# The order in which a scheduled two-layer MLP kernel is written out: TensorE's steps at their planned end

## The chip, the cores and the metric

The kernel runs on one core of a Trainium2 chip. What counts is the device time of one launch in microseconds (us). Five engines work side by side: TensorE (PE in the profile; PEld is its loading of weights), VectorE (DVE), ScalarE (ACT), GpSimd (POOL), and SyncE (SP), which issues the DMAs here.

## The reference

Sliding-window attention feeds two MLPs, one after the other, all in fp32:

```python
scores = scale * (q @ k.T)                 # 4 x 8 heads, 576 positions, head size 64
attn = softmax(scores where 0 <= i - j < 64)
x = (attn @ v) as (2304, 512)
h = x @ w_in                               # layer 0: 512 x 2048
x = (s * relu(h)**2 + b) @ w_out           # 2048 x 512
h = x @ w_in2                              # layer 1
out = (max(h, 0) + alpha * min(h, 0)) @ w_out2
```

What the title calls two layers, the code numbers 0 and 1; the words "layer one" of the change mean the first of them.

## The kernel before

Every fp32 operand is split into a high and a low part, and each product is the sum of three matmuls (high by high, high by low, low by high). So weights are converted on the chip: `converted` loads a piece (`raw`, L676), and ScalarE (L680, L684) and VectorE (L689, L690, L694, L699) split it; `weight_pair` forms sums of weights (L797 to L800) and stages them (L706, L708, L711); `weight` makes the pieces of w_out (ScalarE L769, VectorE L772, GpSimd L764 for a running sum that serves the bias, whose matmuls are L782).

The hidden units are handled in groups: five in layer 0, (0,0) to (0,4), four in layer 1. The tokens are taken in three pieces of 768, each as two halves of 384 columns. From group (0,2) on, `hidden_pair` computes two blocks of hidden units by two halves of tokens with seven products instead of eight (a scheme like Strassen's). Each `product` is six matmuls of 128x384 (L1016). The results lie in PSUM: b1 and b4 are tiles of the pool "h", and T["hb"] is one tile of two banks, "ab" in the profile, half 0 for b2 and half 1 for b3. The copies between them (L1027) are ScalarE's, and `total` (VectorE, L1047 in layer 0, L1049 in layer 1) reads both halves of "ab":

```python
product(6, 2, b2_, hb2, False)
product(2, 3, b1_, b1, False)
copy(b3_, b2_, [hb2], [hb3], 2)
product(7, 4, b3_, hb3, False)
product(3, 5, b2_, hb2, False)
copy(b4_, b3_, [hb3], [b4], 4)
product(4, 6, b4_, b4, False)
```

`project` multiplies the activated blocks by w_out into four PSUM banks y0 to y3 (L1507), and `sums` brings a group's result into the running sum `ay` in SBUF. There are two ways: VectorE adds y to ay (L1601); or, for those m that `CARRIED` names, ScalarE copies ay into the bank before the group (L1500), TensorE accumulates on it, and ScalarE copies it back (L1594).

The order of all this is planned. Each piece of work is a step of `Plan`, with the ways (engine and cost) in which it can be done, what it reads and writes, a due time `at`, and an earliest time. `emit` takes the steps one after the other as a list scheduler does: per engine it plans a start and an end from the costs, and calls the step's function at once, so the program is written in the order of planned starts. The tile framework then derives every wait between engines from the order in which the program was written: of two steps on one tile, with one of them writing it, the later written one waits for the earlier. The queue of each engine runs in its own written order. The due times of conversions done ahead of their group come from `EARLY_AT` and `OUT_AT` and the line in `ahead`.

Of the kernel before, what the change touches and what calls it, by code (L numbers as in the profile page):

```python
# [2 lines left out]

# [28 lines left out]
EARLY = (4, 2, 0, 3, 1, 1, 0)  # L32
# [8 lines left out]
LAG = 1.7  # L41
SEVEN = ((1, 1), (1, 2), (1, 3))
OUT_EARLY = {(0, 3): (0,), (0, 4): (1, 2), (1, 0): (3,), (1, 1): (4,), (1, 2): (5,)}
OUT_AT = {(0, 3): (32.0,), (0, 4): (27.4, 76.1), (1, 0): (53.8,), (1, 1): (27.3,), (1, 2): (51.8,)}
EARLY_AT = {0: (2.3, 28.5, 91), 1: (0,), 2: (39.8,)}
AHEAD2 = 30.0
IDLE = 0.0
PAIRS_ACT = 430.0
CARRIED = {(0, 2): (1,3,), (0, 3): (1,3,), (0, 4): (1,3,)}
LAG7, FORM = 2.3, 10.0  # L50
SOON7 = {(1, 1): (0.0, 0.0, 0.0), (1, 2): (0.0, 0.0, 0.0), (1, 3): (0.0, 0.0, 12.0)}
SOON = 16.0
# [30 lines left out]
class Plan:  # L83
# [100 lines left out]
    def emit(self):  # L184
        n = len(self.steps)
        after = [[] for _ in range(n)]
        for i, (_, deps, _, first, _) in enumerate(self.steps):
            for d in deps + first:
                after[d].append(i)
        path = [0.0] * n  # L190
        for i in range(n - 1, -1, -1):
            cost = min(w[1] + w[3] for w in self.steps[i][0])
            path[i] = cost + max((path[j] + 0.1 for j in after[i]), default=0.0)
        rank = [(-self.steps[i][2], path[i]) for i in range(n)]

        def hop(a, b):

            if a == b:
                return 0.0 if a == "pe" else 0.12
            return 0.2 if "pe" in (a, b) else 0.1  # L200

        took = {}
        left = [len(s[1]) + len(s[3]) for s in self.steps]
        done = [0.0] * n
        free = {"sp": 0.7, "dve": 2.2, "pool": 0.75, "act": 2.0, "pe": 1.1}
        pool_from = 0.0
        ready = {i for i in range(n) if left[i] == 0}
        order = []
        while ready:
            cands = []  # L210
            for i in ready:
                ways, deps, _, _, after_ = self.steps[i]
                best = None
                for w in ways:
                    share = len(w) > 4
                    w = w[:4]
                    t = max((done[d] + hop(took[d], w[0]) for d in deps), default=0.0)
                    t = max(t, free.get(w[0], 0.0), after_)
                    if w[0] == "pe" and t < self.SLOW:
                        w = (w[0], w[1] * 2, w[2], w[3])  # L220
                    if w[0] == "sp" and t < self.SLOW_DMA:
                        w = (w[0], w[1] * self.DMA_FACTOR, w[2], w[3])
                    if share:
                        w = (w[0], w[1] + 0.8 * max(0.0, min(free["pool"], t + w[1]) - max(t, pool_from)), w[2], w[3])
                    value = t + w[1] * (1.0 + self.SPARE[w[0]]) + w[3]
                    if best is None or value < best[0]:
                        best = (value, t, w)
                cands.append((best[1], i, best[2]))
            t0, i0, b0 = min(cands, key=lambda c: (c[0], self.steps[c[1]][2], c[1]))
            t0, i0, b0 = max(  # L230
                (c for c in cands if c[2][0] == b0[0] and c[0] <= t0 + self.WINDOW),
                key=lambda c: (rank[c[1]], -c[1]),
            )
            eng, cost, fn, tail = b0
            free[eng] = t0 + cost
            if eng == "pool":
                pool_from = t0
            done[i0] = t0 + cost + tail
            took[i0] = eng
            ready.remove(i0)  # L240
            order.append((t0, eng))
            fn()
            for j in after[i0]:
                left[j] -= 1
                if left[j] == 0:
                    ready.add(j)
        assert len(order) == n
        return max(done)


@with_exitstack
def tile_window_attention_two_mlps(
# [92 lines left out]
    for g in range(SPLIT[0]):  # L345
        for bi in range(NB):
            n = blocks[bi][1]
            took = len(groups[0][g]) * 24 * n * 0.000444
# [12 lines left out]
    with tc.manual_schedule():  # L361
# [415 lines left out]
        def bias(at):  # L777
            ps = T.tile("bias", h_ps, [P, 512], F32, "h", 2)

            def mms():  # L780
                for m in range(NK):
                    nc.tensor.matmul(T[ps][:, m:m + 1], wsum[:, m * P:(m + 1) * P], b_sb[:, 0:1], start=True, stop=True)  # L782

            T.step([("pe", 1.5, mms, 0.0)], reads=["wsum", "b"], writes=[ps], at=at)
            T.step([dve(NK, lambda: nc.vector.tensor_copy(ybias, T[ps][:, :NK]))], reads=[ps], writes=["ybias"], at=at)
# [54 lines left out]
        def weight_load(n, at):  # L840
            for k in (0, 2, 3, 1):
                lo, hi = PIECES[k]
                w = w_slot(n, k)
                for h in "hl":
                    T.parts[f"{w}.{h}"] = w
                T.step(
                    dma(1, P * (hi - lo) * W2 * 8, lambda w=w, lo=lo, hi=hi: nc.sync.dma_start(
                        out=f32(T[w]), in_=wd[n, :, 2 * lo * W2:2 * hi * W2])),
                    reads=[f"wd.{n}.{k}"], writes=[f"{w}.h", f"{w}.l"], at=at,
                )  # L850
# [689 lines left out]
        def carried(m, layer, g):  # L1540
            return (layer, g) in CARRIED and m in CARRIED[layer, g]

# [69 lines left out]
        for bi in range(NB):  # L1612
            for hp in range(0, NHP, 2 if bi == 0 else 1):
# [4 lines left out]
                else:  # L1618
                    t = begin[0, 0, bi - 1] + (hp / NHP) * (begin[0, 0, bi] - begin[0, 0, bi - 1]) - LEAD
                    at1, at2 = t, t + 1.0  # L1620
                before, after = group(hp // 2 if bi == 0 else bi * NHP + hp, bi, (hp, hp + 1) if bi == 0 else (hp,), at1, at2)
# [26 lines left out]
        for g in range(SPLIT[0]):  # L1648
            for i, f in enumerate(groups[0][g]):
                for part in range(2):  # L1650
                    at = FIRST_W[2 * i + part] if g == 0 else begin[0, g, 0] + (i + 2 * part) * pace[g, 0] - 12.0
# [23 lines left out]
        for x, (layer, g) in enumerate(order_of):  # L1675
            fs = groups[layer][g]
            t = begin[layer, g, turns[layer, g][0]]
            took = NQ * len(fs) / 2 * PAIR
            for p in range(len(fs) // 2):
                n = number[layer, g, p]  # L1680
                at = t + p * PAIR
                if x == 0:
                    weight_pair(n, 0, fs[2 * p], fs[2 * p + 1], at - 20.0, at - 20.0 - AHEAD, True)
                else:
                    weight_load(n, at - 10.0)
            end = layer == 0 and g == len(groups[0]) - 1
            for i, f in enumerate(fs if (layer, g) not in SEVEN else ()):
                at = t + LAG * PAIR + i * PAIR / 4 - 12.0 - 15.0 * end
                weight(layer, f, 1, at, at - AHEAD)
            def ahead():  # L1690
                nonlocal early
                for e in range(EARLY[x]):
                    layer_, g_, p_ = next(k for k, v in number.items() if v == early)
                    at = t + (EARLY_AT[g][e] if layer == 1 else 25.0 + e * took / EARLY[x])
                    weight_pair(
                        early, layer_, *groups[layer_][g_][2 * p_:2 * p_ + 2], at + IDLE * (x > 0),
                        at - (AHEAD2 if layer == 1 and g else 30.0), False, (layer, g) in SEVEN,
                    )
                    early += 1

            def ahead_out():
                if layer == 1:
                    staging.more = 2 * NMAX
                for p, since in zip(OUT_EARLY.get((layer, g), ()), OUT_AT.get((layer, g), ())):
                    out_pair(p, t + since + IDLE, t + since - AHEAD2, (layer, g) in SEVEN)

            if (layer, g) != (1, 0):
                ahead_out()
                ahead()
            if (layer, g) in SEVEN:  # L1710
                seven(layer, g)
                continue
            for q in turns[layer, g]:
                for p in range(len(fs) // 2):
                    hidden_pair(layer, g, q, p)
                if end and q == turns[layer, g][0]:
                    bias(t + PAIR)
                for c in range(2):
                    for i in range(len(fs)):
                        project(layer, g, 2 * q + c, i)  # L1720
                    sums(layer, g, 2 * q + c)
            if (layer, g) == (1, 0):
                ahead()
                ahead_out()
# [55 lines left out]
```

## Time and profile before

| | us |
|---|---|
| median of 3 runs | 842.01 (841.2 to 842.93) |
| the profiled execution | 841.64 |
| its span in the trace | 839.6 |
| TensorE busy | 821.4 (98%) |
| VectorE busy | 702.6 (84%) |
| ScalarE busy | 555.2 (66%) |

The span runs from the first to the last instruction of the trace; the rest of an execution's time lies around it. Busy time counts overlapping instructions of one engine once. A matmul's row gives its time from entry to end; since the next one enters before the last one has ended, the pace of a stream is read from start to start.

### The profile page before, as it was taken

What the parts mean: (1) busy time and instruction counts of PE and PEld (TensorE: products, weight loads), DVE (VectorE), ACT (ScalarE), POOL (GpSimd) and SP (SyncE); (2) the same over time, 40 slices, a digit from 0 to 9 for tenths busy, and PEclk for the clock granted to TensorE, in tenths of its full rate; (3) what the DMA queues carried; (4) which work ended last, traced back from release to release, by engine and by line L of the source; (5) the groups of instructions that cost most, each with busy time, mean ns of one, the idle gap of its engine ahead of it and who ended that gap; (6) DMA issues with size and microseconds to landing.
All of it is one profiled execution on the core that took longest, in us unless ns stands there. A gap on an engine that the chain in (4) does not pass through costs nothing.

```text
span 839.6 us, 15049 instructions
## 1 busy us (share of the span) xinstructions
PE 821.4 (98%) x5481; PEld 768.6 (92%) x5485; DVE 702.6 (84%) x1195; ACT 555.2 (66%) x1249; POOL 105.4 (13%) x117
## 2 busy tenths in 40 slices
PE   7899999999999999999999999999999999999998
PEld 4688887888899999999999999999989999999998
DVE  6977899698995698789949898978799988888695
ACT  6777997644575576778748677775566566656461
POOL 6542355532100001001000000000000000000000
PEclk9999999999999999999999999999999999999999
DMA  8575976476648999989698676998785599469813
GB/s 284 185 231 153 283 229 197 164 261 242 236 170 324 368 342 368 405 311 369 249 388 300 259 314 246 333 363 304 278 301 187 211 328 346 131 212 350 319 47 114
DMA packets 81258, 224.61 MB, mean 268 GB/s; under 512 B 8096, under 2 KB 33824, under 8 KB 81184
## 3 DMA queue, kind: packets, MB, share of 16 engines
q1 hardware_dynamic: 81184, 223.65, 74.2%
q8 instruction: 43, 0.70, 0.3%
q14 instruction: 31, 0.25, 0.1%
HBM read 154.67 MB, written 68.94 MB: 266 GB/s over the span
## 4 chain that ended last, share of the span: by engine, by line
PE 69%; DVE 13%; DMA 12%; ACT 3%; issue 1%; POOL 1%; SPq 0%; DVEq 0%; ACTq 0%; POOLq 0%
PE y L1507 16%; PE h L1016 14%; PE y L1299 13%; PE ab L1016 11%; PE h L1417 7%; DMA raw<-w_out 4%; PE y L1477 3%; DMA raw<-w_in 3%; DMA vd<-al 2%; DVE raw L694 1%; PE ab L531 1%; PE y L636 1%; PE y L605 1%; DVE raw L699 1%; DVE raw L690 1%
## 5 line engine op out<-in xcount | busy, mean ns | idle before, releaser
L1016 PE MATMUL h<-ax,aw 128*128 128x384 f32 x936 | 184.4, 335 | 2.0 <-ACT h L1027 1.2
L1016 PEld LDWEIGHTS h<-ax,aw 128*128 128x128 f32 x936 | 163.9, 188 | 4.1 <-ACT h L1027 1.8
L1507 PE MATMUL y<-ax,woh 128*128 128x384 f32 x672 | 153.9, 335 | 2.3 <-DVE ay L1601 1.8
L1016 PE MATMUL ab<-ax,aw 128*128 128x384 f32 x702 | 139.9, 335 | 1.1 <-ACT ab L1027 0.6
L1016 PEld LDWEIGHTS ab<-ax,aw 128*128 128x128 f32 x702 | 122.9, 188 | 3.0 <-ACT ab L1027 1.6
L1507 PEld LDWEIGHTS y<-ax,woh 128*128 128x128 f32 x672 | 119.3, 188 | 4.2 <-DVE ay L1601 3.3
L1507 PE MATMUL y<-ax,wol 128*128 128x384 f32 x336 | 95.0, 334 | 0.0
L1417 PE MATMUL h<-ax,aw 128*128 128x512 f32 (+1 forms) x360 | 84.3, 377 | 0.8 <-DVE ax L654 0.7
L1417 PEld LDWEIGHTS h<-ax,aw 128*128 128x128 f32 x360 | 61.9, 189 | 12.4 <-DVE ax L654 1.6
L1299 PE MATMUL y<-ax,woh 128*128 128x384 f32 (+1 forms) x273 | 61.7, 333 | 0.0
L1507 PEld LDWEIGHTS y<-ax,wol 128*128 128x128 f32 x336 | 61.5, 188 | 0.0
L1128 ACT ACTIVATE al<-h 128x384 f32<-128x384 f32 (+2 forms) x58 | 30.1, 519 | 40.0 <-PE h L1417 21.6
L680 ACT ACTIVATE raw<-raw 128x512 f32<-128x512 f32 x56 | 37.5, 674 | 21.8 <-DMA raw<-w_in 14.2
L588 POOL TENSOR_TENSOR as__83<-as__83,den 128x512 f32<-128x512 f32 x36 | 41.5, 1173 | 59.9 <-DVE den L581 37.0
L1299 PEld LDWEIGHTS y<-ax,woh 128*128 128x128 f32 x273 | 48.4, 188 | 0.3 <-ACT y L1313 0.3
L1323 DVE TENSOR_TENSOR ay<-y,ay 128x384 f32<-128x384 f32 (+1 forms) x73 | 39.3, 546 | 10.5 <-PE y L1299 6.6
L764 POOL TENSOR_TENSOR al<-al,raw 128x512 f32<-128x512 f32 x15 | 21.8, 1450 | 193.4 <-DVE raw L699 193.4
L694 DVE SCALAR_TENSOR_TENSOR raw<-raw 128x512 int32<-128x512 int32 x56 | 42.9, 773 | 2.9 <-ACT raw L684 2.7
L1299 PE MATMUL y<-ag,wol 128*128 128x384 f32 x192 | 43.9, 335 | 0.4 <-DVE ag L711 0.4
L1313 ACT COPY y<-y 128x384 f32<-128x384 f32 x54 | 25.1, 465 | 27.7 <-PE y L1299 24.2
L1145 ACT ACTIVATE aq<-aq,slope 128x384 f32<-128x384 f32 x48 | 27.2, 610 | 23.9 <-DVE aq L1049 23.8
L570 ACT ACTIVATE as__83<-as__83,nm 128x128 f32<-128x128 f32 x96 | 37.3, 392 | 4.7 <-DVE nm L556 4.5
(189 smaller groups left out, 1670.9 us busy)
## 6 DMA issues: line engine op xcount, KB each, us to landing
ax<-xd SPq DMA_DIRECT2D x91, 768.0 KB, 6.8
aw<-wd SPq DMA_DIRECT2D x33, 512.0 KB, 5.3
xd<-ax SPq DMA_DIRECT2D x21, 768.0 KB, 4.1
raw<-w_in SPq DMA_DIRECT2D x28, 512.0 KB, 5.7
raw<-w_out SPq DMA_DIRECT2D x28, 512.0 KB, 5.6
wd<-ag SPq DMA_DIRECT2D x27, 512.0 KB, 5.0
xd<-aq SPq DMA_DIRECT2D x12, 768.0 KB, 4.2
xd<-ax SPq DMA_DIRECT2D x36, 192.0 KB, 4.7
```

The source lines that it names most:

```text
L570: nc.scalar.activation(sm3()[:, x, :], S_(h)[:, i * P:(i + 1) * P] if summed else sm3()[:, x, :], AF.Exp, bias=T[nm][:, x:x + 1], scale=sc ...
L588: eng.tensor_mul(x, x, d)
L680: [act(512, lambda: nc.scalar.activation(T[t], H().bitcast(F32), AF.Abs, scale=65536.0))],
L694: [dve(512, lambda: nc.vector.scalar_tensor_tensor(out=L(), in0=H(), scalar=-0x80000000, in1=L(), op0=ALU.bitwise_and, op1=ALU.bitwise_or) ...
L1016: nc.tensor.matmul(bank(), W[:, wj, a, kt * P:(kt + 1) * P], X[:, c, kt, :], start=start and kt == 0 and y == 0, stop=kt == 1 and y == 2, ...
L1128: T.step([act(n, lambda: nc.scalar.activation(rn(), hn(), AF.Relu)), dve(n, lambda: nc.vector.tensor_scalar_max(rn(), hn(), 0.0))], reads= ...
L1145: T.step([act(HALF, lambda: nc.scalar.activation(r2n(), hn(), AF.Identity, scale=slope[:, f:f + 1]))], reads=[hk, "side"], writes=[r2], at ...
L1299: nc.tensor.matmul(v(to)[:, c], W[:, s, a * P:(a + 1) * P], G[:, h, c], start=start and p == 0 and y == 0, stop=p == 1 and y == 2, skip_gr ...
L1323: [dve(e.stop - e.start, lambda: nc.vector.tensor_add(T[k][:, e], v(x)[:, e], T[k][:, e]))],
L1417: nc.tensor.matmul(T[ps][:, :n].rearrange("p (c t) -> p c t", t=P), T[w][:, k * P:(k + 1) * P], T[X(x, k)], start=st, stop=sp,)
L1477: nc.tensor.matmul(T[Y(m)][:, :n], T[w[a]][:, m * P:(m + 1) * P], T[gx[c]], start=(x == 0 and j == 0), stop=(x == len(fs) - 1 and j == 2),)
L1507: nc.tensor.matmul(ps, T[w][:, m * P:(m + 1) * P], T[x], start=(i == 0 and j == 0 and not carried(m, layer, g)), stop=(last and j == 2), s ...
```

## The change

It has three parts. `emit` no longer calls a step's function when it picks it, but hands the picked steps to the new `write`. That keeps each engine's own order, and writes the steps in the order of a key: for a step on TensorE its planned end, for all others their planned start. Group (0,2) leaves `CARRIED`, so its y1 and y3 are added by VectorE too. And the due times of weights and w_out pieces that are converted ahead take other values.

```diff
-OUT_AT = {(0, 3): (32.0,), (0, 4): (27.4, 76.1), (1, 0): (53.8,), (1, 1): (27.3,), (1, 2): (51.8,)}
-EARLY_AT = {0: (2.3, 28.5, 91), 1: (0,), 2: (39.8,)}
+OUT_AT = {(0, 3): (27.2,), (0, 4): (24.0, 77.8), (1, 0): (76.9,), (1, 1): (28.4,), (1, 2): (48.2,)}
+EARLY_AT = {0: (14.4, 32.7, 83.6), 1: (0,), 2: (22.3,)}
...
-CARRIED = {(0, 2): (1,3,), (0, 3): (1,3,), (0, 4): (1,3,)}
+CARRIED = {(0, 3): (1,3,), (0, 4): (1,3,)}
...
             order.append((t0, eng))
-            fn()
+            picked.append((i0, b0))
             for j in after[i0]:
                 left[j] -= 1
                 if left[j] == 0:
                     ready.add(j)
         assert len(order) == n
+        self.write(picked, [t for t, _ in order], after)
         return max(done)
+
+    def write(self, picked, begins, after):
+
+        left = [len(s[1]) + len(s[3]) for s in self.steps]
+        then, last, way, key = {}, {}, {}, {}
+        for (i, b), t in zip(picked, begins):
+            way[i] = (t, b)
+            key[i] = t + b[1] if b[0] == "pe" else t
+            if b[0] in last:
+                then[last[b[0]]] = i
+                left[i] += 1
+            last[b[0]] = i
+        heap = [(key[i], i) for i in way if left[i] == 0]
+        heapq.heapify(heap)
+        count = 0
+        while heap:
+            _, i0 = heapq.heappop(heap)
+            t0, (eng, cost, fn, _) = way[i0]
+            count += 1
+            fn()
+            for j in after[i0] + ([then[i0]] if i0 in then else []):
+                left[j] -= 1
+                if left[j] == 0:
+                    heapq.heappush(heap, (key[j], j))
+        assert count == len(way)
...
-                    at = t + (EARLY_AT[g][e] if layer == 1 else 25.0 + e * took / EARLY[x])
+                    at = t + (EARLY_AT[g][e] if layer == 1 else 15.0 + e * took / EARLY[x])
```

The lines of the new kernel from `hidden_pair` on are 28 higher than those of the old one (L1016 becomes L1044). On TensorE there are as many instructions as before, on GpSimd and SP too; VectorE has 15 more and ScalarE 27 fewer. The order is the same up to about 235 us of the old run, and nearly so after about 600 us.

TensorE, at the first pair of that stretch (238 us of the old run): products 7 and 3 on the two halves of "ab", then the next products on "h" tiles, with the queues whose signal each waits for. Before:

```order
L1016 MATMUL ab_2557<-ax_78,aw_80 128x384 [waits DMAHW5_49,Activation_49]
L1016 MATMUL ab_2557<-ax_78,aw_80 128x384 x5
L1016 MATMUL ab_2557<-ax_78,aw_80 128x384 [waits DMAHW7_49]
L1016 MATMUL ab_2557<-ax_78,aw_80 128x384 x5
L1016 MATMUL h_2801<-ax_78,aw_80 128x384 [waits Activation_49]
L1016 MATMUL h_2801<-ax_78,aw_80 128x384 x5
L1016 MATMUL h_2727<-ax_78,aw_80 128x384 [waits DMAHW0_49,Activation_49]
```

And of the changed kernel:

```order
L1044 MATMUL ab_2557<-ax_78,aw_80 128x384 [waits DMAHW5_49,Activation_49]
L1044 MATMUL ab_2557<-ax_78,aw_80 128x384 x5
L1044 MATMUL ab_2557<-ax_78,aw_80 128x384 [waits DMAHW7_49,Activation_49]
L1044 MATMUL ab_2557<-ax_78,aw_80 128x384 x5
L1044 MATMUL h_2799<-ax_78,aw_80 128x384 x6
L1044 MATMUL h_2728<-ax_78,aw_80 128x384 [waits DMAHW0_49]
```

The order of TensorE is the same; product 3 waits for ScalarE now, and the two products behind it no longer do.

VectorE, at the sums of the second half of group (0,2) (277 us of the old run; L797 to L800 form sums of weights, L708 and L711 stage them). Before, where y1 and y3 go by ScalarE:

```order
L800 TENSOR_TENSOR as__83<-raw_84,as__83 128x256
L711 TENSOR_TENSOR ag_81<-raw_84,ag_81 128x256
L708 CAST ag_81<-as__83 128x2x256
L1118 CAST ax_78<-al_86 128x384
L1601 TENSOR_TENSOR ay_79<-y0_3008,ay_79 128x384
L1121 TENSOR_TENSOR ax_78<-al_86,ax_78 128x384
L1601 TENSOR_TENSOR ay_79<-y2_3016,ay_79 128x384
```

And of the changed kernel:

```order
L739 TENSOR_TENSOR ag_81<-raw_84,ag_81 128x256
L736 CAST ag_81<-as__83 128x2x256 x2
L739 TENSOR_TENSOR ag_81<-as__83,ag_81 128x2x256 x2
L1629 TENSOR_TENSOR ay_79<-y0_3012,ay_79 128x384
L1629 TENSOR_TENSOR ay_79<-y1_3016,ay_79 128x384
L1149 TENSOR_TENSOR ax_78<-al_86,ax_78 128x384
L1629 TENSOR_TENSOR ay_79<-y2_3021,ay_79 128x384
L1629 TENSOR_TENSOR ay_79<-y3_3025,ay_79 128x384
```

The half's four sums stand close together, and a burst of weight steps stands ahead of them in both orders, a longer one in the new.

SP, the DMA queue at the beginning of that stretch (raw is a load of weights, ax one of a layer's input, wd a store of staged weights). Before:

```order
L676 DMA raw_84<-w_in1 128x1024 x2
L979 DMA ax_78<-xd_87 128x1536 x7
L823 DMA wd_89<-ag_81 128x1024
L823 DMA wd_89<-ag_81 128x512
L823 DMA wd_89<-ag_81 128x1024 x2
L676 DMA raw_84<-w_in1 128x1024 x3
```

And of the changed kernel:

```order
L704 DMA raw_84<-w_in1 128x1024 x2
L1007 DMA ax_78<-xd_87 128x1536
L851 DMA wd_89<-ag_81 128x1024
L704 DMA raw_84<-w_in1 128x1024
L1007 DMA ax_78<-xd_87 128x1536 x4
L851 DMA wd_89<-ag_81 128x512
L851 DMA wd_89<-ag_81 128x1024 x2
```

A load of weights that stood behind the seven loads of ax and four stores is now ahead of most of them.

## Rows read from the trace of the kernel before

**Rows 1.** The page: its head and its first part, the busy time by engine.
```profile
span 839.6 us, 15049 instructions
...
PE 821.4 (98%) x5481; PEld 768.6 (92%) x5485; DVE 702.6 (84%) x1195; ACT 555.2 (66%) x1249; POOL 105.4 (13%) x117
```

**Rows 2.** The table by stretch: start:end and length, then each engine's busy time (instructions), clock granted.
```profile
235.00:332.00 97.00, 95.21 (x541) 93.49 (x540) 74.67 (x142) 59.34 (x120) 3.98 (x3) 1.00 0.87 324
235.00:835.20 600.20, 594.42 (x3400) 587.37 (x3398) 501.29 (x874) 388.35 (x756) 9.48 (x7) 1.00 0.78 287
```

**Rows 3.** Timeline of PE around 238 us: start, busy time, operation, count, [idle before, releaser].
```profile
237.48 2.24 PE L1016 MATMUL ab<-ax,aw 128*128 128x384 f32 x12
239.56 1.37 PE L1016 MATMUL h<-ax,aw 128*128 128x384 f32 x7
```

**Rows 4.** Timeline of ACT in that stretch.
```profile
239.75 0.46 ACT L1027 COPY h<-ab 128x384 f32<-128x384 f32 x1 [1.02 <-PE ab L1016]
```

**Rows 5.** Timeline of PE, 390 to 396 us.
```profile
390.22 1.21 PE L1016 MATMUL ab<-ax,aw 128*128 128x384 f32 x6
391.98 1.31 PE L1016 MATMUL h<-ax,aw 128*128 128x384 f32 x6 [0.55 <-ACT h L1027]
...
394.29 0.61 PE L1507 MATMUL y<-ax,woh 128*128 128x384 f32 x2 [0.48 <-DVE ay L1601]
...
395.44 0.95 PE L782 MATMUL h<-b_sb,al 128*128 128x1 f32 x8
396.25 0.59 PE L1507 MATMUL y<-ax,woh 128*128 128x384 f32 x2
```

**Rows 6.** Timeline of ACT at 391 us.
```profile
391.46 0.46 ACT L1027 COPY h<-ab 128x384 f32<-128x384 f32 x1 [1.07 <-PE ab L1016]
```

**Rows 7.** Timeline of PE around 18 us.
```profile
18.69 1.90 PE L636 MATMUL y<-ay 128*64 128x64 f32 x56
```

**Rows 8.** Timeline of ACT and of DVE around 21 us.
```profile
20.86 0.38 ACT L649 CAST ax<-y 128x256 fp32r<-128x256 f32 x1
...
21.27 0.42 DVE L650 CAST ax<-y 128x256 fp32r<-128x256 f32 x1
```

**Rows 9.** Timeline of all engines at the end.
```profile
834.86 0.50 PE L1299 MATMUL y<-ax,wol 128*128 128x192 f32 x3
...
835.20 0.50 PE L1299 MATMUL y<-ax,woh 128*128 128x192 f32 x3
...
836.07 0.62 DVE L1323 TENSOR_TENSOR ay<-y,ay 128x192 f32<-128x192 f32 x2 [0.76 <-PE y L1299]
```

**Rows 10.** Timeline of PE, 276 to 280 us and 326 us.
```profile
276.05 1.21 PE L1016 MATMUL ab<-ax,aw 128*128 128x384 f32 x6
277.46 0.61 PE L1507 MATMUL y<-ax,woh 128*128 128x384 f32 x2 [0.21 <-ACT y L1500]
...
279.92 0.35 PE L1507 MATMUL y<-ax,woh 128*128 128x384 f32 x1
...
326.69 0.61 PE L1507 MATMUL y<-ax,woh 128*128 128x384 f32 x2 [1.35 <-DVE ay L1601]
```

**Rows 11.** Timeline of DVE, 276 to 279 us.
```profile
276.81 0.42 DVE L711 TENSOR_TENSOR ag<-raw,ag 128x256 fp32r<-128x256 f32 x1
...
277.75 0.55 DVE L1601 TENSOR_TENSOR ay<-y,ay 128x384 f32<-128x384 f32 x1
```

**Rows 12.** Groups of ACT by line, 235 to 332 us: busy, mean ns, idle before.
```profile
L680 ACT ACTIVATE raw<-raw 128x512 f32<-128x512 f32 x10 | 6.7, 669 | 5.2 <-DMA raw<-w_in 5.2
...
L1500 ACT COPY y<-ay 128x384 f32<-128x384 f32 x12 | 5.5, 496 | 1.3 <-DVE ay L1559 1.2
L1594 ACT COPY ay<-y 128x384 f32<-128x384 f32 x10 | 4.8, 475 | 0.1
```

**Rows 13.** Groups of DVE by line, the same stretch.
```profile
L1601 DVE TENSOR_TENSOR ay<-y,ay 128x384 f32<-128x384 f32 x10 | 5.4, 549 | 11.6 <-PE y L1507 11.6
```

**Rows 14.** The chain that ended last, 235 to 332 us: start, length, what.
```profile
253.88 12.90 DMA raw<-w_in
```

More of the change, by code (lines that the diff above doesn't have):

```diff
@@ L1 @@
+import heapq
 import struct
@@ L208, in emit @@
         order = []
+        picked = []
         while ready:
```

## The prediction

> **What bounds the kernel now.** The reader first takes the page's head: TensorE is busy for 98% of an 839.6 us span, VectorE for 84%, ScalarE for 66% [rows 1]. The table by stretch then says where anything is left: from 235 to 835.2 us TensorE is busy for 594.42 of 600.20 us at the full clock, so it idles for 5.78 us in all [rows 2]. So from 235 us on, where the change mostly lies, there is no other engine to relieve: each new wait of TensorE is paid nearly in full, and the most that can be won is its few remaining waits.
>
> What a wait costs is more than its idle time. Twelve matmuls of 128x384 take 2.08 us from start to start, 0.173 each [rows 3]. Six that start at 390.22 should be followed at 391.26; the next six start at 391.98 [rows 5], 0.72 us late, of which the timeline shows 0.55 as idle, because the last matmul's tail counts as busy. And these six, the first after a wait, take 1.31 us where the six before took 1.21 [rows 5]: another 0.10. One wait of this form costs **0.82 us**, that is, its idle time and 0.27 more.
>
> The wait itself is told by the timelines of TensorE and ScalarE together. `hidden_pair` gives seven products to TensorE in the order 1, 5, 6, 2, 7, 3, 4. Product 7 fills half 1 of the tile "ab", product 3 half 0, and the copy h<-ab reads half 1. At 238 us products 7 and 3 are the twelve matmuls at 237.48 [rows 3]; product 7 ends about 238.7, product 3 about 239.7, and ScalarE, idle for 1.02 us, starts its copy at 239.75 [rows 4]: it waited for product 3, which it doesn't read. At 391 us the same copy starts at 391.46 after 1.07 us of idleness [rows 6], and there product 4 is next on TensorE and waits for it: that is the 0.72 us. So a wait follows the order in which the program is written, over the whole tile.
>
> **The change, part by part.** *The order of writing.* A step of TensorE is now written at its planned end. No engine's own order changes by that; what changes is which side of a pair of steps on one tile waits. At ten places of the new order (about 238, 249, 391, 454, 531, 582, 621, 680, 769 and 796 us of the old run) the copy h<-ab now comes before product 3. ScalarE is free about 1 us sooner. But product 3, next on TensorE after product 7, must now wait for the copy. It is the chain of 391 us, one product earlier: product 7's end, a copy of 0.46 us, then the matmul, and I take the same 0.82 us. The places:
> - 238, 454, 680, 769, 796: the copy finds ScalarE free; 5 x 0.82 = 4.1 us.
> - 249 and 531: other ScalarE steps stand ahead of the copy, one of the kind of L680, which takes 0.669 us [rows 12]; I add about half such a step: 2 x 1.25 = 2.5.
> - 391 and 582: product 4's wait goes and product 3's comes: 0.
> - 621: ScalarE is late there already, and TensorE waits on either side; half a price, 0.4 (bounds 0 and two prices).
>
> Two places lie outside the pairs. In the first attention block, eight of the 56 matmuls at 18.69 [rows 7] now wait for the cast that ScalarE does from 20.86 to 21.24; VectorE's cast at 21.27 [rows 8] follows them. Eight at 1.90/56 us are 0.27, with two handovers about 0.5 us, in a stretch where TensorE waits for VectorE: +0.5. At the end, the last six matmuls of 128x192, from 835.20, now wait for the sum of the first half. That half ends at about 835.36, and one of the two sums takes about 0.35 us (both 0.62) [rows 9], so the six start at about 835.8, 0.6 later and 0.1 slower; then one sum instead of two is left, 0.27 less: +0.44.
>
> Together 4.1 + 2.5 + 0.4 + 0.5 + 0.44 = **7.9 us**, with bounds 5.5 (the two late places as the clean ones, 621 free, a third of the clean ones absorbed by waits that follow anyway) and 9.5 (621 at two prices, the start at 1).
>
> The Trainium skill says, in "TensorE: Matmul & The Clock Gate", section "Step-by-step: what each phase is for", that the next weights are loaded while matmuls run; by that alone a restart would be free, a wait 0.72 and the sum 7.1. The 1.31 against 1.21 us [rows 5] disagrees, and I keep the trace's.
>
> *Sums of group (0,2) no longer carried.* 12 copies into PSUM (L1500, 0.496 us) and 12 out of it (L1594, 0.475 us) leave ScalarE, 11.7 us [rows 12]; 12 additions of 0.549 us come to VectorE, 6.6 us [rows 13]. VectorE is busy for 74.67 of that stretch's 97 us [rows 2], so 6.6 us fit beside TensorE on the whole. TensorE waits for an addition only where it needs the bank again: an addition must be done before the same bank's next matmuls, and if it stands behind conversions it is late.
>
> *Other times for conversions and out pairs.* The same loads, ScalarE and VectorE steps stand elsewhere in three queues (SP, ScalarE, VectorE); POOL's order is the same. Four waits depend on what stands ahead of a sum or of the bias. At 277 us the addition at 277.75 stood behind a burst of weight steps such as L711 at 276.81 [rows 11], and TensorE needed 3.87 us from 276.05 to 279.92 for 15 matmuls worth 2.60 [rows 10]: 1.27 lost. The new order has four additions there, still behind such a burst, without copies on ScalarE. At 326 us 1.35 + 0.27 = 1.6 [rows 10]; at 394 us 0.48 + 0.27 = 0.75; at 395.4 the bias takes 0.81 for eight matmuls of one column [rows 5]. Bursts stand ahead of these places in the new order too, with other lengths, so I take half of each as won: 0.6 + 0.8 + 0.4 + 0.4, **-2.2 us**. The bounds: -6.5, if every wait between 235 and 575 us that is not counted above went (by the rule of idle time plus 0.27 they come to that); +3, if none went and nearly half of the 6.6 us of additions came late. I stay below zero, near the middle of the gains, since the stretch as a whole has time for the additions; no further than that, since conversions are moved and none is saved: loads of w_in, one of which held the chain for 12.90 us [rows 14], are queued on SP behind other loads than before.
>
> Sum: 7.9 - 2.2 = +5.7 us. The profiled execution took 841.64 us around its span of 839.6; it would take 847.3. The median of the runs is 842.01, 0.37 above it: **847.7 us**.
>
> **The rivals.**
> *Faster: the released ScalarE pays.* ScalarE was held 1.0 us and more at each such copy, and has 11.7 us less to do [rows 4, 12]. If its later steps come so much sooner that nearly all remaining waits go, the gain is 5.78 us of idleness plus 0.27 for each of some 20 waits, less the two that are only moved and the bias's own work: about 9 us. With the lower 5.5 for the new waits: 842.0 + 5.5 - 9 = 838.5. It decides once over 7.2 us of old waits go. Against it: at 326 and 394 us TensorE waits for VectorE [rows 5, 10], which gets more to do.
> *The new wait doesn't bind.* The Trainium skill, "PSUM — Partial Sum Buffer", section "PSUM bank collisions raise a hardware error", has engines work side by side as long as they are in different banks, and the tile's halves are different banks. If the new wait falls away, what is left is the start, the end and the moved conversions, 842.0 + 0.9 - 2.2 = 840.7 us. The copy at 239.75 [rows 4] speaks against it: it did wait for the other half.
> *Nothing to see.* The new waits at 5.5, the old ones won at 5.5: 842.0.
> *Slower still.* No old wait goes, and a quarter of the added additions' 6.6 us lands on TensorE: 842.0 + 7.9 + 1.6 = 851.5.
>
> **How the numbers follow.** A measurement can tell 0.2%, 1.7 us: faster is below 840.3, slower above 843.7. Forecast 0.57, for itself from 844 to 850.5; faster by ScalarE 0.14; no binding wait 0.03; nothing to see 0.12; slower still 0.14. That makes faster 0.14, same 0.03 + 0.12 = 0.15, slower 0.57 + 0.14 = 0.71. The range of 8 in 10 runs from 840.0, which leaves nearly all of the faster cases out, to 852.5, a little past the slower rival.
>
> **What would show it.** Right: at 238, 454, 680, 769 and 796 us TensorE stands idle some 0.55 us ahead of product 3, released by ScalarE's copy h<-ab, and ScalarE's copy starts right at product 7's end; no wait of product 4 at 391 and 582; a wait of some 0.5 us ahead of the last six matmuls; ScalarE without copies L1500 and L1594 of group (0,2). Wrong: product 3 following product 7 without a gap; or TensorE's idleness after 235 us below the 5.78 of now, which would mean that the old waits went faster than new ones came; or new waits of TensorE for VectorE's sums between 235 and 330 us, which would mean that the second sum is positive.

## The result and the profile after

The changed kernel takes 849.79 us (median of 5 runs, 848.59 to 852.72), the kernel before 841.20 in its 5 runs; the ratio is 1.0104, 95% interval 1.0082 to 1.0127. It is **slower by 1%**, as forecast in sign, and 2.1 us above the forecast's 847.7. The profiled execution is the shortest of the five (848.59 us, granted clock 1.00 on average; the longest, 852.72 us, shows 0.995), so the medians lie 8.6 us apart and the spans, which are read below, 7.2. The page's head of the changed kernel:

```profile
span 846.8 us, 15040 instructions
...
PE 821.8 (97%) x5485; PEld 769.3 (91%) x5485; DVE 711.7 (84%) x1210; ACT 545.4 (64%) x1222; POOL 106.9 (13%) x117
```

The span is 7.2 us longer, with the same TensorE work. The table by stretch shows where (the second row runs to the last stretch's end, as [rows 2]):

```profile
235.00:332.00 97.00, 92.83 (x527) 91.14 (x527) 83.12 (x160) 52.84 (x105) 5.71 (x4) 1.00 0.87 321
235.00:842.40 607.40, 594.81 (x3402) 588.18 (x3401) 510.61 (x891) 380.03 (x733) 11.81 (x8) 1.00 0.78 284
```

After 235 us TensorE idles for 607.40 - 594.81 = 12.59 us, where it idled for 5.78 [rows 2]. VectorE is busier in the first stretch (83.12 us for 74.67), with no loss there from it, as we shall see. The list of waits names the one that grew. First the kernel before, then the changed one (engine, tile and line, what is waited for; us in total, times, longest):

```profile
PE ab L1016 <- ACT h L1027: 0.2, 1, 0.2
```

```profile
PE ab L1044 <- ACT h L1055: 11.3, 11, 1.8
```

Product 3's wait for the copy h<-ab has gone from 0.2 us to 11.3 us of idleness. In TensorE's timeline these are the places (the first row is product 7, at the place of [rows 3]):

```profile
238.20 1.21 PE L1044 MATMUL ab<-ax,aw 128*128 128x384 f32 x6
239.96 0.81 PE L1044 MATMUL ab<-ax,aw 128*128 128x384 f32 x3 [0.55 <-ACT h L1055]
...
251.37 0.44 PE L1044 MATMUL ab<-ax,aw 128*128 128x384 f32 x1 [1.75 <-ACT h L1055]
...
284.60 0.62 PE L1044 MATMUL ab<-ax,aw 128*128 128x384 f32 x2 [1.76 <-ACT h L1055]
...
393.68 0.79 PE L1044 MATMUL ab<-ax,aw 128*128 128x384 f32 x3 [1.00 <-ACT h L1055]
...
459.32 0.81 PE L1044 MATMUL ab<-ax,aw 128*128 128x384 f32 x3 [1.34 <-ACT h L1055]
...
627.24 0.61 PE L1044 MATMUL ab<-ax,aw 128*128 128x384 f32 x2 [1.36 <-ACT h L1055]
...
685.35 1.32 PE L1044 MATMUL ab<-ax,aw 128*128 128x384 f32 x6 [0.61 <-ACT h L1055]
...
775.05 1.15 PE L1044 MATMUL ab<-ax,aw 128*128 128x384 f32 x5 [0.61 <-ACT h L1055]
```

At 239.96, 685.35 and 775.05 (and at 586.54 and 802.99, the same) the wait is the clean one. At 251.37, 284.60, 393.68, 459.32 and 627.24 it is longer. ScalarE's timeline tells the two kinds apart:

```profile
282.96 0.67 ACT L708 ACTIVATE raw<-raw 128x512 f32<-128x512 f32 x1 [3.69 <-DMA raw<-w_in]
283.54 0.63 ACT L712 ACTIVATE raw<-raw 128x512 int32<-128x512 uint32 x1
284.08 0.47 ACT L1055 COPY h<-ab 128x384 f32<-128x384 f32 x1
...
458.39 0.49 ACT L1528 COPY y<-ay 128x384 f32<-128x384 f32 x1
458.81 0.46 ACT L1055 COPY h<-ab 128x384 f32<-128x384 f32 x1
...
684.83 0.46 ACT L1055 COPY h<-ab 128x384 f32<-128x384 f32 x1 [0.64 <-PE ab L1044]
```

At 684.83 the copy starts as soon as product 7 has ended, and product 3 0.52 us after the copy's start. At 284.08 the copy stands behind a weight's conversion (L708, L712) that itself had waited 3.69 us for a load of w_in, and so TensorE waits for that load too, though twelve matmuls of y filled the first part of the gap after product 7. At 458.81 it stands behind copies of the carried sums. Counted from start to start of matmuls (each should follow the one ahead by 0.173 us), product 3 loses 0.83 us at 238, 0.88 at four more clean places, 1.3 to 2.0 at six, and 0.2 to 0.4 at two where other products fill in: **14.8 us at 13 places**.

The waits for sums are gone. At the two places of [rows 10], now at 280.59 and 329.44 us, the matmuls of y follow the six of product 7 at their pace, 1.04 us after those began, and the last of the twelve starts 1.91 us later (TensorE's timeline of the changed kernel):

```profile
279.55 1.20 PE L1044 MATMUL ab<-ax,aw 128*128 128x384 f32 x6
280.59 0.51 PE L1535 MATMUL y<-ax,woh 128*128 128x384 f32 x2
...
282.50 0.34 PE L1535 MATMUL y<-ax,wol 128*128 128x384 f32 x1
...
328.40 1.20 PE L1044 MATMUL ab<-ax,aw 128*128 128x384 f32 x6
329.44 0.51 PE L1535 MATMUL y<-ax,woh 128*128 128x384 f32 x2
...
331.35 0.34 PE L1535 MATMUL y<-ax,wol 128*128 128x384 f32 x1
```

VectorE's group there, now 20 additions [rows 13]:

```profile
L1629 DVE TENSOR_TENSOR ay<-y,ay 128x384 f32<-128x384 f32 x20 | 10.5, 553 | 3.4 <-PE y L1535 3.4
```

The start and the end came much as forecast. In the first block TensorE's last sixteen matmuls wait for ScalarE, where the forecast had eight, and VectorE's cast comes at 22.14 in place of 21.27 [rows 7, 8]:

```profile
18.41 1.39 PE L664 MATMUL y<-ay 128*64 128x64 f32 x42
21.34 0.69 PE L664 MATMUL y<-ay 128*64 128x64 f32 x16 [1.54 <-ACT ax L677]
```

```profile
22.14 0.42 DVE L678 CAST ax<-y 128x256 fp32r<-128x256 f32 x1 [0.79 <-PE y L664]
```

At the end the last six matmuls wait for the first half's sum, and one sum is left behind them [rows 9] (timeline of all engines):

```profile
841.90 0.50 PE L1327 MATMUL y<-ax,wol 128*128 128x192 f32 x3
...
842.85 0.58 PE L1327 MATMUL y<-ax,woh 128*128 128x192 f32 x3 [0.45 <-DVE ay L1351]
...
843.80 0.36 DVE L1351 TENSOR_TENSOR ay<-y,ay 128x192 f32<-128x192 f32 x1 [1.01 <-PE y L1327]
```

The balance after 235 us, from start to start: TensorE lost 12.2 us before, and loses 19.2 now. Of the 19.2, product 3 has 14.8 and the tail 0.7; 3.6 are left of the old 12.2. With 0.7 from the start and 0.27 saved on the last sum that is 7.4, against 7.2 of span. The start's 0.7 (product 7 at 238.20 in place of 237.48 us) is that of one execution: in the traces of the other runs that are written at planned ends there (2, 3, 6 and 10 below) the same matmul starts between 237.54 and 239.03 us.

### The profile page after: what moved, and what is told of

It is laid out like the page before. It is cut to its first block, busy times and chain, and to the rows that moved or that the text cites. A ratio compares the mean times of both kernels' runs of the same rounds, so it can differ in the third digit from the quotient of the medians.

```text
span 846.8 us, 15040 instructions
## 1 busy us (share of the span) xinstructions
PE 821.8 (97%) x5485; PEld 769.3 (91%) x5485; DVE 711.7 (84%) x1210; ACT 545.4 (64%) x1222; POOL 106.9 (13%) x117
## 4 chain that ended last, share of the span: by engine, by line
PE 77%; DVE 10%; DMA 6%; ACT 4%; issue 1%; POOL 1%; SPq 0%; ACTq 0%; POOLq 0%; DVEq 0%
PE y L1535 20%; PE h L1044 16%; PE y L1327 13%; PE ab L1044 12%; PE h L1445 7%; PE y L1505 3%; DMA vd<-al 2%; DMA raw<-w_in 2%; PE y L664 1%; PE ab L559 1%; DMA al<-w_in 1%; PE y L633 1%; DVE raw L722 1%; DVE raw L727 1%; DVE raw L718 1%
## 5 line engine op out<-in xcount | busy, mean ns | idle before, releaser
L1044 PE MATMUL h<-ax,aw 128*128 128x384 f32 x936 | 184.3, 335 | 0.6 <-DVE raw L1176 0.4
L1044 PEld LDWEIGHTS h<-ax,aw 128*128 128x128 f32 x936 | 164.2, 188 | 1.5 <-DVE raw L1176 0.7
L1044 PE MATMUL ab<-ax,aw 128*128 128x384 f32 x702 | 142.3, 337 | 11.5 <-ACT h L1055 11.3
L1044 PEld LDWEIGHTS ab<-ax,aw 128*128 128x128 f32 x702 | 122.6, 188 | 16.1 <-ACT h L1055 15.6
L708 ACT ACTIVATE raw<-raw 128x512 f32<-128x512 f32 x56 | 37.8, 679 | 26.2 <-DMA raw<-w_in 19.2
L792 POOL TENSOR_TENSOR al<-al,raw 128x512 f32<-128x512 f32 x15 | 23.6, 1575 | 189.6 <-DVE raw L727 189.6
L727 DVE CUSTOM_DVE_ANT_0 raw<-raw 128x1024 uint16<-128x1024 uint16 x56 | 40.9, 737 | 0.2
```

Source lines behind the costliest of these rows:

```text
L708: [act(512, lambda: nc.scalar.activation(T[t], H().bitcast(F32), AF.Abs, scale=65536.0))],
L727: [dve(512, lambda: nc.vector.tensor_tensor(ti(), ti(), L(), op=ALU.add), port=True)],
L1044: nc.tensor.matmul(bank(), W[:, wj, a, kt * P:(kt + 1) * P], X[:, c, kt, :], start=start and kt == 0 and y == 0, stop=kt == 1 and y == 2, ...
```

## The experiments

All times are medians, each with runs of the kernel before beside it, which took 841.5 to 841.9 us there; a ratio is taken against those, with its 95% interval, and need not be the quotient of the two medians. The theory: the loss is product 3's wait for a copy that shares its tile, and nothing else of the change loses.

**1. The changed kernel, written in the order of planned starts.**

```diff
-        self.write(picked, [t for t, _ in order], after)
+        for _, b in picked:
+            b[2]()
```

> The changed kernel with its steps written in the order of planned starts, as the kernel before does it; the carried sums and the other times stay changed. My theory: product 3's waits (14.8 us after 235 us in the changed run), the tail's 0.5 and the start's 0.7 go, the two waits of product 4 near 391 and 585 us return (1.7): 849.8 - 14.3 = 835.5 us (834 to 838), faster than the kernel before. Rival (the moved conversions and the added additions carry the loss, and the order of writing only moves waits): 846 us or more.

Measured: 838.96 us, ratio 0.9970 (0.9954 to 0.9986). The order of writing makes the difference of 11 us, and the rest of the change is a gain. It is 3.5 us less of a gain than I had expected, and outside the range given. TensorE's idleness after 235 us:

```profile
235.00:831.00 596.00, 591.71 (x3400) 587.65 (x3399) 509.10 (x890) 378.18 (x731) 11.55 (x7) 1.00 0.79 289
```

That is 4.3 us, and counted from start to start 8.2 us, where the changed kernel had 3.6 besides product 3 and the tail. Waits for the held copy h<-ab, as that of product 4 in the kernel before, come to 3.3 us at four places (251, 281, 328 and 580 us), where I had put 1.7 at two. And the trace has a wait for VectorE's sum at 393 us (0.74) and one for a ScalarE copy at 625 us (1.3) that the changed kernel doesn't have: there, product 3's waits stand ahead of them, in which the other engines could catch up. That last reading fits the numbers, and wasn't tried by itself.

**2. The kernel before, with the new order of writing alone.**

```diff
-            fn()
+            picked.append((i0, b0))
...
+        self.write(picked, [t for t, _ in order], after)
```

> The kernel before with the new order of writing alone. My theory: product 3 waits at about ten places, 0.8 us where ScalarE is free and more where its queue is late, with old waits for VectorE kept: 8 to 15 us over the kernel before, 849 to 856 us. Rival: within 2 us of the kernel before.

Measured: 849.61 us, ratio 1.0086 (1.0058 to 1.0113). So the order of writing makes either kernel some 8 to 11 us slower, and the rival is out.

**3 and 4. Product 3 alone.** In run 3 every TensorE step but product 3 of `hidden_pair` is written at its planned end; in run 4 product 3 is the only one that is. The order on each engine is the changed kernel's in both.

```diff
-                T.step(
+                i = T.step(
                     pe(6, HALF, mms), ...
                 )
+                if j == 3:
+                    T.marked.add(i)
...
-            key[i] = t + b[1] if b[0] == "pe" else t
+            key[i] = t + b[1] if b[0] == "pe" and i not in self.marked else t     # run 3
+            key[i] = t + b[1] if i in self.marked else t                          # run 4
```

> The changed kernel, with product 3 of the pairs alone written at its planned start, all other steps of TensorE at their planned end. My theory: product 3 waits for no copy, product 4's two waits return, start and tail stay: 849.8 - 14.8 + 1.7 = 836.7 us (835 to 839.5). Rival (other steps written at their end cost it): 845 us or more.

> The changed kernel, with product 3 of the pairs alone written at its planned end, all other steps of TensorE at their planned start. My theory: nearly the whole loss is there: 849.8 less the start's 0.7 and the tail's 0.5, 848.6 us (846.5 to 850.5). Rival (other steps cost it): near the run with all steps at their start, 836.

Measured: run 3 840.25 us, 0.9982 (0.9964 to 1.0000); run 4 849.66 us, 1.0094 (1.0068 to 1.0120). One product of the seven carries the whole loss: run 4 is the changed kernel's time. (Run 4's trace also has 3.4 us at half the clock behind its longest wait, see the last section, and neither the start's nor the tail's wait.) The lists of waits, of run 3 and then of run 4 (the line numbers are shifted):

```profile
PE h L1045 <- ACT h L1058: 1.7, 2, 1.1
...
PE ab L1045 <- ACT h L1058: 0.4, 1, 0.4
```

```profile
PE ab L1045 <- ACT h L1058: 11.1, 12, 1.9
```

Run 3 again comes out some 3.5 us above my figure and a little above its range, and its trace shows waits like those of run 1: 3.2 us from start to start for held copies at 253, 330, 583 and 653 us, 0.7 for a sum at 396 and 1.2 for a ScalarE copy at 628.

**5 and 6. No shared tile.** The two halves of "ab" become two PSUM tiles of one bank each from the first pair on, so that the copy and product 3 need not wait for each other in either order. `total` becomes two VectorE instructions of half the width, in the same step. Run 5 does this to run 1's kernel, run 6 to the changed kernel.

```diff
-            b2_, b3_ = (lambda: T["hb"][:, 0, :HALF]), (lambda: T["hb"][:, 1, :HALF])
+            b2_, b3_ = (lambda: T["hb", 0][:, :HALF]), (lambda: T["hb", 1][:, :HALF])
...
+            a_pool.close()
+            b_ps = ctx.enter_context(tc.tile_pool(name="b_ps", bufs=1, space=bass.MemoryType.PSUM))
             for x in range(2):
+                T.made["hb", x] = b_ps.tile([P, 512], F32, tag=f"ab{x}", name=f"ab{x}", bufs=1)
```

> The run with planned starts (838.96 us, its reference here), with the two halves of ab as two PSUM tiles of one bank each, so that the copy h<-ab and product 3 have no wait on each other in either order; total becomes two VectorE instructions of 128x384 instead of one of 128x768. My theory: the copy starts at product 7's end; the waits of product 4 and of the next pairs for it (four of 0.6 to 0.8 us plus 0.1 each in that run, 3.3 us) mostly go: 836.5 us (835 to 838.5). Rival (those waits come from ScalarE's queue alone): 839.

> The changed kernel (planned ends) with the two halves of ab as two PSUM tiles and total as two instructions. My theory: the loss is the wait between the halves, so it goes although all steps are still written at their planned ends; start 0.7 and tail 0.5 stay: 837.7 us (836 to 840). Rival (a wait for ScalarE's copy is needed anyway, or late writing costs elsewhere): 845 or more.

Measured: run 5 836.68 us, 0.9926 (0.9902 to 0.9950); run 6 837.93 us, 0.9936 (0.9912 to 0.9960). Run 6 differs from the changed kernel by the tiles and the two halves of `total` alone, and 12 us are gone (the split of `total`, which only adds to VectorE's work, wasn't tried by itself). Its timelines around 676 us, of TensorE and then of ScalarE, show why:

```profile
675.62 2.24 PE L1045 MATMUL ab<-ax,aw 128*128 128x384 f32 x12
677.70 0.68 PE L1329 MATMUL y<-ax,aw 128*128 128x384 f32 x3
```

```profile
676.91 0.46 ACT L1056 COPY h<-ab 128x384 f32<-128x384 f32 x1 [0.63 <-PE ab L1045]
```

The twelve matmuls of products 7 and 3 run without a gap, product 7 ends about 676.8, and the copy starts at 676.91 while product 3 writes the other bank. So the wait was one of the program, not of the memory; here the trace agrees with the Trainium skill, "PSUM — Partial Sum Buffer", section "PSUM bank collisions raise a hardware error", by which two engines can work at the same time in different banks. **Run 5 beats both kernels**: TensorE idles for 2.7 us after 235 us,

```profile
235.00:829.00 594.00, 591.28 (x3392) 586.65 (x3391) 511.09 (x929) 380.01 (x733) 11.39 (x8) 1.00 0.79 290
```

**7 and 8. The other two parts alone.** Run 7 is the kernel before with group (0,2) out of `CARRIED`, run 8 the kernel before with the new values of `OUT_AT` and `EARLY_AT` and 15.0 for 25.0.

```diff
-CARRIED = {(0, 2): (1,3,), (0, 3): (1,3,), (0, 4): (1,3,)}
+CARRIED = {(0, 3): (1,3,), (0, 4): (1,3,)}
```

> The kernel before with group (0,2) out of CARRIED and nothing else changed. By the forecast's own parts: of the waits at 277, 326, 394 us and the bias (4.4 us) those at 277 and 326 are touched, half of them go: 840.5 us against 841.9 (839 to 842.5). Rival (the 12 additions come late): 843 or more. If the whole gain of the run with planned starts were due to this part: 839.

> The kernel before with the new values of OUT_AT, EARLY_AT and 15.0 alone. Moved conversions take part of the waits away and bring others: 841 us against 841.9 (838.5 to 843.5). If the whole gain of the run with planned starts were due to this part: 839. Rival (the new times fit only with the other parts): 843 or more.

Measured: run 7 850.72 us, 1.0079 (1.0050 to 1.0108), a clear miss; run 8 840.77 us, 0.9977 (0.9959 to 0.9996). Apart one loses 9 us and the other wins 1 (7 and 2 by the ratios); together (run 1) they win 2.9 (2.5). In run 7 TensorE waits for one sum for 5.17 us. TensorE's row, then VectorE's rows ahead of it:

```profile
402.74 1.01 PE L1507 MATMUL y<-ax,woh 128*128 128x384 f32 x2 [5.17 <-DVE ay L1601]
```

```profile
398.51 1.64 DVE L1121 TENSOR_TENSOR ax<-al,ax 128x384 fp32r<-128x384 f32 x1
400.08 0.74 DVE L772 SCALAR_TENSOR_TENSOR wol<-raw,s_sb,woh 128x512 fp32r<-128x512 f32 x1
400.74 0.41 DVE L689 TENSOR_SCALAR raw<-raw 128x512 f32<-128x512 f32 x1
401.19 0.43 DVE L690 TENSOR_SCALAR raw<-raw 128x512 int32<-128x512 int32 x1
401.53 0.69 DVE L694 SCALAR_TENSOR_TENSOR raw<-raw 128x512 int32<-128x512 int32 x1
402.13 0.55 DVE L1601 TENSOR_TENSOR ay<-y,ay 128x384 f32<-128x384 f32 x1
```

The sum at 402.13 stands behind a burst of conversions (L772 to L694) and an L1121 that took 1.64 us, where its group takes 0.58 on average (GpSimd's L764 ran beside it; whether that slowed it wasn't tried). At 367 us there is one more wait, 3.1 us from start to start, behind conversions whose load of w_in came late. Leaving out the carried sums also moved the conversions: the two loads of w_in that SP issues at 331.6 and 332.2 us in the kernel before are issued at 342.3 and 342.7 here. With the new times as well (run 1) the longest wait for a sum after 235 us is 0.75 us. So these runs give no price for either part by itself.

**9 and 10. The tiles in the kernel before, and the sums in the changed one.** Run 9 is the kernel before with the tiles of runs 5 and 6. Run 10 is the changed kernel with group (0,2) back in `CARRIED`.

> The kernel before, with nothing changed but the two halves of ab as two PSUM tiles and total as two VectorE instructions. My theory: its copies h<-ab are no longer held until product 3's end, so product 4's waits at 392 and 583 us (0.82 + 0.88) go, and little else: 841.6 - 1.7 = 839.9 us (838.5 to 841). Rival (the held copies also make ScalarE late elsewhere, so more goes): 837 or less. Second rival (VectorE's longer total eats it): 841.5 or more.

> The changed kernel with group (0,2) back in CARRIED: order of writing and times changed, sums not. Product 3 still waits for the copy, so it stays slow; with the order of planned starts the sums together with the times were worth 840.8 - 839.0 = 1.8 us. My theory: 849.8 + 1.8 = 851.6 us (848.5 to 854). Rival (the carried sums of the change make the loss): 845 or less.

Measured: run 9 840.54 us, 0.9986 (0.9965 to 1.0006): its two waits of product 4 are gone from the trace, but the gain can't be told from none. Run 10 847.81 us, 1.0078 (1.0062 to 1.0095): slow, as it should be while product 3 waits, and 2 us faster than the changed kernel where I expected 2 us slower and gave 848.5 as the least. Neither difference is clear: the intervals of run 10 and of the changed kernel overlap, and so do those of runs 1 and 8, from whose medians I had taken the sums' worth of 1.8 us. Run 10's list of waits says where its trace differs from the changed kernel's, which has 11.3 us in this line:

```profile
PE ab L1044 <- ACT h L1055: 8.8, 12, 1.4
```

From start to start product 3 loses 12.4 us there instead of 14.8 (the two longest waits, at 251 and 284 us behind loads of w_in, are not there, and some stand elsewhere), and all else 5.1 instead of 4.4. So the sums and product 3's waits can't be added up as separate terms either: the sums change how late the copies are.

## Why the prediction was right, and where its terms were not

- *What bounds the kernel*: right. Every wait of TensorE after 235 us went into the span: 7.0 us more of them, 7.4 with the start and the last sum, against 7.2 us more span.
- *The mechanism*: right, and shown by runs 3, 4 and 6: product 3 behind a copy of the other half of its tile.
- *The price where ScalarE is free*, 0.82 us: 0.83 at 238 and 0.88 at four places.
- *The sum of the new waits*, 7.9 us with bounds to 9.5: wrong in size. Product 3's 14.8, less 1.7 for product 4's two waits that go, with start 0.7 and tail 0.46, are **14.3 us**. (My bounds don't even add up: the terms named give 5.3 and 9.7, where I wrote 5.5 and 9.5.) Two steps failed. First, the places: I counted ten, and there are thirteen. At 284.60, 331.79 and 443.66 twelve matmuls of y stand between products 7 and 3, and the copy is later than they are (2.6 us in all). Second, the price where other ScalarE steps stand ahead of the copy, "about half such a step": product 3 inherits the whole lateness of ScalarE's queue and of the loads that queue waits for. The place I called 621 lost 1.6 us for the 0.4 taken, 249 lost 2.0 for 1.25, 454, which I took for clean, 1.6 for 0.82, and 391 1.3 for 0.82; only 531 came as priced (1.3 for 1.25).
- *Start and end*, 0.5 and 0.44: 0.7 (in this one trace) and 0.46.
- *The old waits*, -2.2 with a bound of -6.5: also wrong in size. 12.2 - 3.6 = 8.6 us of them went, 6.9 without product 4's two. I took half of four waits; the three for sums went whole (3.6 us), and others past 575 us went too. Most of it is owed to the sums and the other times together: with planned starts (run 1) 8.2 us are left, 3.3 of them for held copies, so 5.6 of the 6.9 go there too, and some 1.3 only hide behind product 3's waits.
- Sum: +14.3 - 6.9 = +7.4, where I had +7.9 - 2.2 = +5.7. The two errors have opposite signs, so the total came out nearer than its terms. That the time lies in the range is owed in part to this, and this part is luck.
- *The rivals*: the released ScalarE did not pay. It needed 7.2 us of old waits to go, and 6.9 went, nearly all; it failed on the new waits, 14.3 us where it took 5.5. That the new wait doesn't bind is refuted for this program, and is what run 6 shows once the tiles are apart. The late additions of "slower still" did not come in the changed kernel, but did in run 7, at 5.17 us.

## What to carry to other kernels

When a framework derives waits from the order in which a program is written, moving one step in that order swaps who waits, over as much as the framework takes for one object: look for pairs on one tile that touch different parts of it, and give each part its own tile before tuning the order (worth 12 us under the new order here, and nothing clear under the old one, run 9). Price a wait not by its handover alone but by the queue of the engine it waits for, with the loads that queue waits for. And parts of a retuned plan (due times, the way sums are kept) should be priced together, since here each moved the others' work (runs 7, 8 and 10).

## What the runs showed of the hardware

The granted clock fell after some waits. Run 7, table by stretch: TensorE idle from 364.2 to 367.1 and for 5.17 us before 402.7, and what followed (the columns are those of [rows 2], the granted clock third from the end):

```profile
364.00:367.10 3.10, 0.18 (x2) 0.00 (x0) 2.67 (x6) 3.10 (x7) 0.00 (x0) 1.00 0.88 346
367.10:371.60 4.50, 4.48 (x17) 4.42 (x18) 4.47 (x11) 3.89 (x10) 0.00 (x0) 0.62 0.98 327
...
394.00:402.70 8.70, 3.42 (x18) 3.10 (x18) 8.12 (x14) 5.53 (x12) 1.86 (x1) 0.97 0.97 361
402.70:412.50 9.80, 9.76 (x33) 9.52 (x34) 8.10 (x15) 3.42 (x5) 1.29 (x1) 0.51 0.99 398
```

The first stretch after the wait shows 0.62 of the full 2.4 GHz and the second 0.51 for 9.8 us, that is the level of 1.2 GHz; matmuls of 128x384 follow each other by 0.32 us there instead of 0.173. So a wait of 5.17 us cost about as much again. In run 2 a shorter one did it too:

```profile
326.80:328.70 1.90, 0.05 (x1) 0.00 (x0) 1.90 (x4) 0.46 (x1) 0.50 (x1) 1.00 1.00 401
328.70:332.60 3.90, 3.89 (x13) 3.89 (x14) 1.74 (x4) 0.99 (x2) 0.00 (x0) 0.56 0.94 353
332.60:336.00 3.40, 3.40 (x22) 3.40 (x21) 2.54 (x4) 1.72 (x4) 0.00 (x0) 1.00 0.50 158
```

The clock was 0.56 for 3.9 us, and whole again behind that, after an idle time of 1.86 us, while in the changed kernel it stayed at 1.00 after idle times of 1.75 and 1.76 us at 251 and 284 us. In run 4 it was 0.50 from 251.8 to 255.2 us, behind an idle time of 1.92 us. These lengths are no rule: in the first block the changed kernel and run 6 have the same wait of 1.54 us, ended at 21.34 and at 21.38 us, and the clock fell behind it in run 6 alone. The changed kernel, then run 6:

```profile
23.10:26.50 3.40, 3.04 (x45) 2.20 (x45) 3.33 (x8) 3.14 (x7) 2.62 (x5) 1.00 0.50 183
```

```profile
23.10:26.50 3.40, 3.40 (x26) 2.47 (x30) 3.33 (x7) 3.08 (x7) 2.62 (x5) 0.50 0.51 174
```

What decides it these runs leave open. I had priced a wait of TensorE by its length and the first matmuls behind it; no wait after 235 us in the kernel before had shown more.
